# Output projection of a two-branch layer: token blocks 2 and 3 computed with seven block products in place of eight

## The chip, the cores and the metric

The kernel runs on one core of a Trainium2 chip. The core has a matrix engine (TensorE, PE in the profile; its weight loads are the row PEld), three engines for elementwise work (VectorE = DVE, ScalarE = ACT, GpSimd = POOL), a queue that issues transfers (SyncE = SP) and 16 DMA engines. SBUF is the on-chip working memory with 128 partitions; PSUM holds eight banks of 128 x 512 float32 values, into which TensorE accumulates. The metric is the device time of one execution in microseconds (us).

## The reference, cut to what matters

x has 2048 tokens of 640 channels. A linear-attention branch and an MLP branch read the same normalised x, and both are added to x.

```python
xn = _layernorm(x)
# branch A: q, k, v, two softmaxes per head, linear attention -> o (2048 x 640)
o = num / den
A = o.transpose(0, 2, 1, 3).reshape(B, S, D) @ wo          # wo: 640 x 640
# branch B: layernorm, 640 -> 1728, gelu, 1728 -> 640
return x + A + B_
```

The change lies in the product with `wo`, the last work of the kernel.

## The kernel before, in words

Tokens are handled in four blocks b = 0..3 of 512 columns, channels in KC = 5 bands of 128 partitions. Everything is kept transposed (channels on partitions, tokens along the row), so the projection is, for output band m of block b, the sum over bands c of `wo[c, m]` transposed times `o[c]`. Float32 accuracy is kept by splitting each operand into a high part, which has the reduced format float32r, and a low part, the rest. `mm3` (L70, L71, L72) issues the three products high x high, high x low and low x high for one pair of bands, each a 128 x 128 by 128 x 512 matmul. A column of the projection is one (b, m): five such triples, fifteen matmuls, into one PSUM bank; the columns use banks 6 and 7 in turn (`pw_`). VectorE then adds the bank to `acc[b][:, m]` (L1424), which holds x plus the MLP so far, and SyncE stores that column (L1425). The very last column is cut into two halves of 256 tokens.

The work just ahead of the projection is the end of the MLP: group g = 6, blocks 2 and 3, second matrix. There each output band takes five matmuls (L70 to L72 and L326, L327) into banks 5, 6, 7 in turn, and VectorE adds the bank to `acc` (L331). The fifth band of block 3 is the fourteenth use of this ring and takes bank 5 again, two uses after band 1 of block 3; the first projection column takes bank 6, which band 2 of block 3 held.

Four kinds of work run beside the projection:
- `Attention.split` makes the high part of a band on ScalarE (L1284) and its low part on VectorE (L1286). Block 0's and block 1's are made from `tf` tiles, blocks 2's and 3's from `acc` tiles.
- For block 3 the attention's quotients are still being finished: VectorE takes a reciprocal of `dt` (L1247), transfers spread it over the tile `rx` (L1248 to L1257), VectorE shuffles it (L1263) and GpSimd multiplies it into the result `ob` (L1265), band by band.
- The `acc` of blocks 0 and 1 comes back from memory (L1290) into the tiles that the splits have just read.
- In the last pass, `load_wo` fetches the high and low parts of `wo` (L1296, L1298).

What sets the order: PE, DVE, ACT and POOL run in the order in which the program emits their instructions (`manual_schedule`). The program emits along TensorE's work: after each triple it calls `mlp.tick()`, and a step registered with `mlp.after(n, ...)` is emitted n ticks later. A tick is thus a place in each engine's queue and no time: an engine goes on to its next instruction as soon as that one's data are there, however far TensorE has come. SyncE's queue alone is ordered by a planner from its own estimate of times.

Of the kernel before, what the change touches and what calls it, by code (L numbers as in the profile page):

```python
# [8 lines left out]
F32 = mybir.dt.float32  # L9
F32R = mybir.dt.float32r  # L10
AF = mybir.ActivationFunctionType
ALU = mybir.AluOpType
# [3 lines left out]
P = 128  # L16
S, D, F, H, DH = 2048, 640, 1728, 32, 20
KC = D // P
NB = S // 512
# [27 lines left out]
def f(ap):  # L47
    return ap.bitcast(F32)
# [3 lines left out]
def tile_kernel(ctx: ExitStack, tc: tile.TileContext, x, xT, wkT, wqT, wv, wphi, wo, w1, b1, w2, b2,  # L52
                ident, mmask, emask, vsel, out):
    nc = tc.nc
# [14 lines left out]
    def mm3(ps, lh, ll, rh, rl, first, last, **kw):  # L69
        nc.tensor.matmul(ps, lh, rh, start=first, stop=False, **kw)  # L70
        nc.tensor.matmul(ps, lh, rl, start=False, stop=False, **kw)  # L71
        nc.tensor.matmul(ps, ll, rh, start=False, stop=last, **kw)  # L72
# [25 lines left out]
    acc = [None] * NB  # L98
# [4 lines left out]
    banks = ctx.enter_context(tc.tile_pool(name="banks", bufs=1, space=PSUM))  # L103
# [13 lines left out]
    rp = ys.enter_context(tc.tile_pool(name="raw", bufs=1))  # L117
    wp = ys.enter_context(tc.tile_pool(name="w", bufs=1))

    def mtile(i, dtype=F32):  # L120
        return mp.tile([P, 2, D if i < 5 else 512], dtype, name=f"m{i}")
    y = {}

    def load_x(ts, xp, tag="xb"):
        xbs = []
        for t in ts:
            xb = xp.tile([P, D], F32, name=tag)
            nc.sync.dma_start(xb, x[t * P:(t + 1) * P, :])
            xbs.append(xb)
        return xbs  # L130
# [386 lines left out]
    mlp = Mlp((0, 1, 2, 3), ((0, 2), (1, 3)))  # L517
# [8 lines left out]
    x0 = load_x(range(2), xp)  # L526
    nc.sync.dma_start(idt, ident)
    wc, parts, dmas = {}, {}, {}
# [23 lines left out]
    x1 = load_x(range(4, 8), xp)  # L552
# [330 lines left out]
    a = ExitStack()  # L883
# [228 lines left out]
    t1 = sp.tile([VM, 5, 480], F32, name="t1")  # L1112
# [198 lines left out]
    wol, phs = [], []  # L1311
    ep = rx = None
# [20 lines left out]
    at = {}  # L1333
# [21 lines left out]
    ep = ctx.enter_context(tc.tile_pool(name="eB", bufs=1, side="right", reuse_waits="tile"))  # L1355
# [35 lines left out]
    w2t, parts = mlp.take_pair(6, True, 3)  # L1391
# [13 lines left out]
    finish(before)  # L1405
    load_ob(1)

    pw_ = Banks(6, 7)
    step = 0
    for b in range(NB):  # L1410
        oh, ol = at[b].oh, at[b].ol
        for m in range(KC):
            ms = slice(m * P, (m + 1) * P)

            for cols in [slice(0, 512)] if (b, m) != (NB - 1, KC - 1) else [slice(0, 256), slice(256, 512)]:
                pw = pw_()[:, cols]
                for c in range(KC):
                    mm3(pw, wol[0][c][:, ms], wol[1][c][:, ms], oh[:, c, cols], ol[:, c, cols], c == 0, c == KC - 1)
                    step += 1
                    mlp.tick()  # L1420
                    for n, at_ in enumerate((3, 28, 53), 1):
                        if step - at_ in range(KC + 1):
                            at[n].split(step - at_, nc.vector)
                nc.vector.tensor_tensor(acc[b][:, m, cols], pw, acc[b][:, m, cols], op=ALU.add)  # L1424
                nc.sync.dma_start(out[ms, b * 512 + cols.start:b * 512 + cols.stop], acc[b][:, m, cols])  # L1425


_INS = ["x", "xT", "wkT", "wqT", "wv", "wphi", "wo", "w1", "b1", "w2", "b2", "ident", "mmask", "emask", "vsel"]
# [60 lines left out]
```

## Time and profile before

| what | value |
|---|---|
| median of 3 runs | 713.96 us (712.85 to 714.65) |
| profiled execution, its own time | 713.46 us |
| its span, first to last instruction | 711.6 us |
| TensorE busy | 703.8 us, 99% of the span |
| DVE, ACT, POOL busy | 514.0, 342.0, 421.4 us |
| granted TensorE clock | 1.000 |
| projection: first matmul | 639.76 us from the span's start |
| last column added | 708.27 us |

The page's columns: a row of the timeline has the start in us from the span's start, the duration in us, the engine, the line, the operation, the tile written and the tiles read, the shapes, how many equal instructions are merged in the row, and in brackets how long the engine had been idle before it and what ended that. A busy TensorE is not TensorE at its peak, and a matmul's recorded duration overlaps the next; the distance between starts is its cost.

### The profile page before, as it was taken

The numbers are of one execution on the slowest core, as the hardware profiler recorded it, in microseconds if no ns is written. First come the engines' busy times: TensorE is split into PE (matmuls) and PEld (weight loads), VectorE is DVE, ScalarE is ACT, GpSimd is POOL, SyncE is SP. The second block draws the span as 40 slices with busy tenths as digits, with TensorE's granted clock in tenths as the row PEclk, the third lists the DMA queues.
The fourth block names the chain that finished last, engine by engine and source line by source line (L and its number), as shares of the span: only waits on it lengthen the run. The fifth ranks groups of instructions, "written<-read, shape, count | busy, mean of one in ns | idle before, by whom it ended". The sixth has DMA issues, their size and how long they took to land. (4 is left out here: it accounts for less than half of the span.)

```text
span 711.6 us, 9745 instructions
## 1 busy us (share of the span) xinstructions
PE 703.8 (99%) x3381; PEld 592.2 (83%) x3381; DVE 514.0 (72%) x821; ACT 342.0 (48%) x563; POOL 421.4 (59%) x360
## 2 busy tenths in 40 slices
PE   9999999999999999999999999999999999999998
PEld 7878888888888888888888888888887878888886
DVE  7777755988754788788888878657769695784622
ACT  6434554444334545545544546367665766450100
POOL 3521314577245997898787879468679787540400
PEclk9999999999999999999999999999999999999999
DMA  9823643485621228236401609964355568446222
GB/s 325 288 72 109 193 121 98 155 266 172 214 105 74 93 75 245 70 110 199 99 0 32 159 1 349 227 191 127 115 162 153 164 187 296 164 127 214 84 80 74
DMA packets 65767, 106.56 MB, mean 150 GB/s; under 512 B 7462, under 2 KB 31814, under 8 KB 63838
## 3 DMA queue, kind: packets, MB, share of 16 engines
q1 hardware_dynamic: 65414, 105.93, 46.5%
q8 instruction: 26, 0.43, 0.2%
q14 instruction: 23, 0.19, 0.1%
q10 hardware_dynamic: 304, 0.01, 0.0%
HBM read 71.37 MB, written 34.55 MB: 149 GB/s over the span
## 5 line engine op out<-in xcount | busy, mean ns | idle before, releaser
L906 PE MATMUL bank<-wkh,y 128*128 128x512 f32 (+1 forms) x480 | 139.5, 364 | 0.0
L70 PE MATMUL bank<-y,w 128*128 128x512 f32 (+1 forms) x294 | 114.2, 389 | 0.0
L71 PE MATMUL bank<-y,w 128*128 128x512 f32 (+1 forms) x294 | 113.7, 387 | 0.0
L72 PE MATMUL bank<-y,w 128*128 128x512 f32 (+1 forms) x294 | 113.6, 386 | 0.0
L64 POOL TENSOR_TENSOR w<-r,w 128x640 fp32r<-128x640 f32 x32 | 52.2, 1645 | 96.0 <-ACT w L61 67.0
L70 PE MATMUL bank<-m,w 128*128 128x512 f32 x260 | 102.3, 394 | 1.1 <-DVE acc L331 0.8
L71 PE MATMUL bank<-m,w 128*128 128x512 f32 x260 | 101.3, 390 | 0.9 <-DVE m L461 0.9
L72 PE MATMUL bank<-m,w 128*128 128x512 f32 x260 | 101.3, 390 | 0.0
L906 PEld LDWEIGHTS bank<-wkh,y 128*128 128x128 f32 x480 | 87.5, 188 | 13.3
L906 PE MATMUL bank<-wkl,y 128*128 128x512 f32 (+1 forms) x240 | 87.4, 364 | 0.0
L70 PEld LDWEIGHTS bank<-y,w 128*128 128x128 f32 x294 | 55.2, 188 | 11.7 <-issue 0.4
L72 PEld LDWEIGHTS bank<-y,w 128*128 128x128 f32 x294 | 55.2, 188 | 11.3
L71 PEld LDWEIGHTS bank<-y,w 128*128 128x128 f32 x294 | 55.2, 188 | 10.9
L942 ACT ACTIVATE m<-m,rs_all 128x1280 f32<-128x1280 f32 x32 | 43.7, 1365 | 42.9 <-POOL m L941 42.8
L70 PEld LDWEIGHTS bank<-m,w 128*128 128x128 f32 x260 | 48.8, 188 | 11.9 <-DVE acc L331 1.0
L944 DVE TENSOR_REDUCE sm<-m 128x64 f32<-128x1280 f32 x32 | 47.4, 1481 | 15.0 <-ACT m L942 14.8
L71 PEld LDWEIGHTS bank<-m,w 128*128 128x128 f32 x260 | 48.8, 188 | 11.1 <-DVE m L461 1.4
L906 PE MATMUL bank<-w,y 128*128 128x512 f32 x240 | 57.4, 391 | 0.0
L72 PEld LDWEIGHTS bank<-m,w 128*128 128x128 f32 x260 | 48.8, 188 | 10.2
L941 POOL TENSOR_TENSOR m<-m,mx 128x640 f32<-128x640 f32 (+2 forms) x48 | 44.4, 939 | 19.2 <-DVE mx L930 19.2
L331 DVE TENSOR_TENSOR acc<-bank,acc 128x512 f32<-128x512 f32 x70 | 46.9, 683 | 11.1 <-PE bank L72 5.9
L906 PEld LDWEIGHTS bank<-w,y 128*128 128x128 f32 x240 | 44.4, 188 | 8.5
(184 smaller groups left out, 1447.2 us busy)
## 6 DMA issues: line engine op xcount, KB each, us to landing
r<-in_w SPq DMA_DIRECT2D x52, 320.0 KB
e<-e SPq DMA_DIRECT2D x40, 256.0 KB
e<-acc SPq DMA_DIRECT2D x52, 160.0 KB
acc<-in_xT SPq DMA_DIRECT2D x4, 1280.0 KB
t<-t SPq DMA_DIRECT2D x8, 512.0 KB
tf<-t SPq DMA_DIRECT2D x2, 1536.0 KB
xb<-in_x SPq DMA_DIRECT2D x8, 320.0 KB
t<-in_x SPq DMA_DIRECT2D x8, 320.0 KB
```

Source lines behind the costliest of these rows:

```text
L64: eng.tensor_tensor(lo, src, f(hi), op=ALU.subtract)
L70: nc.tensor.matmul(ps, lh, rh, start=first, stop=False, **kw)
L71: nc.tensor.matmul(ps, lh, rl, start=False, stop=False, **kw)
L72: nc.tensor.matmul(ps, ll, rh, start=False, stop=last, **kw)
L331: nc.vector.tensor_tensor(acc[b][:, m, :], pw, acc[b][:, m, :], op=ALU.add)
L906: nc.tensor.matmul(ps, lh[:, kc, c], rh[:, kc], start=n == 0, stop=n == 3 * KC - 1)
L941: subs[n, t] = nc.gpsimd.tensor_tensor(ep[:, s], a, b, op=ALU.subtract)
L942: exps[n, t] = nc.scalar.activation(e, e, AF.Exp, scale=rs_all[:, t:t + 1])
L944: nc.vector.tensor_reduce(sm, e.rearrange("p s (h f) -> p (s h) f", f=DH), axis=AX, op=ALU.add)
```

## The change

Blocks 0 and 1 are projected as before. For blocks 2 and 3 the five bands are parted into four and one. The four input bands c = 2q + i and the four output bands m = 2k + j, with q, k, i, j in 0..1, make for each q and k a 2 x 2 block matrix out of `wo` (its blocks a11, a12, a21, a22; the first index is the output's parity, the second the input's), and the two token blocks make the 2 x 2 matrix b11 (block 2, even band), b21 (block 2, odd band), b12 and b22 (block 3). Its product is formed by the variant of Strassen's method with seven block products:

- sums of `wo`: s1 = a21 + a22, s2 = s1 - a11, s3 = a11 - a21, s4 = a12 - s2
- differences of the attention output ("turned forms"): t1 = b12 - b11, t2 = b22 - t1, t3 = b22 - b12, t4 = b21 - t2
- products a11 b11, a12 b21, s1 t1, s2 t2, s3 t3, a22 t4, s4 b22; the partial sums are kept in banks `a`, `b`, `c`, and a bank is read and added to `acc` at several stages of its accumulation.

The fifth input band is added by `rest` as one triple for each output column, and the fifth output band is a whole column as before, in two halves for block 3.

The new supporting work, with its ticks counted from the first triple of the projection:
- tick 1, `load_sums`: one transfer of 4 x 512 columns of `wo`, 1 MB, into tile `w1` (L1412).
- ticks 12 to 18, `add`: the four sums on GpSimd, in place in `w1` (L1424 of the new program, 512 elements in each partition).
- ticks 20 to 26, `hi_sum` and `lo_sum`: their high parts on ScalarE (L1427) and low parts on VectorE (L1431).
- ticks 42 to 60: eight differences on GpSimd (`combine`, L1440). For each, ScalarE writes the high part twice (`turn_hi`, L1456), once to SBUF and once to PSUM bank 3 or 4, and VectorE subtracts to get the low part (`turn_lo`, L1461), reading its first operand from that bank.
- Block 3's split begins at tick 59; before it began at 53.

Lines of the new program that stand for old ones: L1481 and L1518 for the addition L1424, L1482 and L1520 for the store L1425.

```diff
+    def load_sums():
+        sums.append(wp.tile([P, 4, D], F32, name="w1").rearrange("p i d -> p (i d)")[:, :4 * 512])
+        nc.sync.dma_start(sums[0].rearrange("p (c n) -> p c n", c=4), wo[:4 * P, :512].rearrange("(c p) n -> p c n", p=P))
...
+    def add(i):
...
+        o, x0, x1, op = ((a22, a21, a22, ALU.add), (a21, a11, a21, ALU.subtract), (a11, a22, a11, ALU.subtract), (a12, a12, a11, ALU.subtract))[i]
+        nc.gpsimd.tensor_tensor(o, x0, x1, op=op)
+    def hi_sum(c):
+        nc.scalar.activation(sums[1][:, c * 512:c * 512 + 512], sums[0][:, c * 512:c * 512 + 512], AF.Copy)
+    def lo_sum(o, w):
+        at_ = slice(o, o + w)
+        nc.vector.tensor_tensor(lo_part(o)[:, :w], sums[0][:, at_], f(sums[1][:, at_]), op=ALU.subtract)
...
+        nc.gpsimd.tensor_tensor(o, x0, x1, op=ALU.subtract)
...
+        bank = copies()
+        for o in (parts[0], bank):
+            nc.scalar.activation(o.rearrange("p (t q n) -> p t q n", q=4, t=4), src, AF.Copy)
...
+        nc.vector.tensor_tensor(lo, bank, f(hi), op=ALU.subtract)
...
+    steps = [(1, load_sums)]
+    steps += [(12 + 2 * i, lambda i=i: add(i)) for i in range(4)]
+    steps += [(20 + c, lambda c=c: hi_sum(c)) for c in range(4)]
...
+    for n, t in ((1, 3), (2, 28), (3, 59)):
+        steps += [(t + c, lambda n=n, c=c: at[n].split(c, nc.vector)) for c in range(KC + 1)]
+    for t, step in sorted(steps, key=lambda e: e[0]):
+        mlp.after(t, step)
...
+    for k in range(2):
+        place("a", k, k)
+        product("a", k, "a11", "b11", True)
+        read("a", k, 0, 2, False)
+        place("c", k, (2, 5)[k])
+        product("c", k, "a12", "b21", True)
+        rest("c", k, 0, 2)
+        read("c", k, 0, 2)
+    column(2, 4, [2])
+    for k in range(2):
+        place("b", k, (5, 2)[k])
+        product("b", k, "s1", "t1", True)
+        read("b", k, 1, 3, False)
+        product("a", k, "s2", "t2")
+        read("a", k, 0, 3, False)
+        place("c", k, (2, 5)[k])
+        product("c", k, "a22", "t4", True)
+        rest("c", k, 1, 2)
+        read("c", k, 1, 2, False)
+        product("a", k, "s3", "t3")
+        read("a", k, 1, 2)
+        product("b", k, "s4", "b22")
+        rest("b", k, 0, 3)
+        read("b", k, 0, 3)
+        rest("a", k, 1, 3)
+        read("a", k, 1, 3)
+    column(3, 4, [0, 5], (slice(0, 256), slice(256, 512)))
```

SyncE's queue near the end of the MLP, the difference between the two programs: `d`, `o` and `dt` are the denominators and late rows of block 3's attention, `w_6048` is the tile `w1` that takes `wo`.

```order
 L1240 DMA d_98<-acc_5547 4x2560
 L1240 DMA d_98<-acc_5547 2x2560
+L1412 DMA w_6048<-in_wo 128x4x512
 L1244 DMA acc_5547<-o_83 4x2560
 L1242 DMA dt<-d_98 128x128
```

The planner has put the load of `wo` between the two stores of the denominators and the loads that follow them; it waits only for the last matmul that read `w1` (L308 of block 3).

GpSimd's queue from the end of the MLP to its end: `m` is the last hidden tile of the MLP (L314), `acc_5165` and `acc_5547` are the results of blocks 2 and 3, `e` are free tiles.

```order
 L314 TENSOR_TENSOR m_5924<-m_5893,m_5924 64x512
 L1265 TENSOR_TENSOR acc_5165<-acc_5165,rx 128x512
-L1265 TENSOR_TENSOR acc_5547<-acc_5547,rx 128x512 x5
-L1485 UNCONDITIONAL_BRANCH
-L1485 ISA
+L1424 TENSOR_TENSOR w_6048<-w_6048 128x2x2x128 x4
+L1265 TENSOR_TENSOR acc_5547<-acc_5547,rx 128x512 x4
+L1440 TENSOR_TENSOR acc_5165<-acc_5547,acc_5165 128x512
+L1265 TENSOR_TENSOR acc_5547<-acc_5547,rx 128x512
+L1440 TENSOR_TENSOR acc_5165<-acc_5547,acc_5165 128x512
```

The four sums now stand directly behind the last product of block 2 and wait for the load alone; the differences stand among and behind the products of block 3.

VectorE's queue from the third column of block 1 on, before (`tf` is block 1's sum, `acc_4122` block 2's, `y` the split's parts):

```order
L1424 TENSOR_TENSOR tf_6086<-bank_6208,tf_6086 128x512
L1424 TENSOR_TENSOR tf_6086<-bank_6230,tf_6086 128x512
L1424 TENSOR_TENSOR tf_6086<-bank_6249,tf_6086 128x512
L1286 TENSOR_TENSOR y_6278<-acc_5547,y_6277 128x512 x2
L1424 TENSOR_TENSOR acc_4122<-bank_6267,acc_4122 128x512
L1286 TENSOR_TENSOR y_6278<-acc_5547,y_6277 128x512 x3
```

The same place now (`m` and `e` are the parts of the turned forms):

```order
L1481 TENSOR_TENSOR tf_6091<-bank_6226,tf_6091 128x512
L1481 TENSOR_TENSOR tf_6091<-bank_6248,tf_6091 128x512
L1461 TENSOR_TENSOR m_6267<-bank_6268,m_6267 128x512
L1461 TENSOR_TENSOR m_6283<-bank_6284,m_6283 128x512
L1461 TENSOR_TENSOR m_6296<-bank_6297,m_6296 128x512
L1481 TENSOR_TENSOR tf_6091<-bank_6273,tf_6091 128x512
L1461 TENSOR_TENSOR m_6311<-bank_6312,m_6311 128x512
L1518 TENSOR_TENSOR acc_4122<-bank_6307,acc_4122 128x512
L1461 TENSOR_TENSOR m_6325<-bank_6326,m_6325 128x512
L1518 TENSOR_TENSOR acc_4122<-bank_6321,acc_4122 128x512
```

The eight low parts of the turned forms stand between the additions of the columns, and block 3's split comes behind them.

More of the change, by code (lines that the diff above doesn't have):

```diff
@@ L1406, in tile_kernel @@
     load_ob(1)
[L1408 to L1411, printed above, removed]
-        for m in range(KC):
[L1413 to L1425, printed above, removed]
+    sums, turned = [], {}
@@ new lines, in lo_sum, with combine @@
+    def lo_sum(o, w):
+        at_ = slice(o, o + w)
+        nc.vector.tensor_tensor(lo_part(o)[:, :w], sums[0][:, at_], f(sums[1][:, at_]), op=ALU.subtract)
+    def combine(i, q):
+        c0, c1 = 2 * q, 2 * q + 1
+        x = {(b, c): at[b].ob[:, c] for b in (2, 3) for c in (c0, c1)}
+        t = {j: turned[j, q][0] for j in (1, 2, 3, 4) if (j, q) in turned}
+        o = ep.tile([P, 512], F32, name="e", bufs=6) if i in (2, 3) else x[2, c0 if i == 1 else c1]
+        x0, x1 = {1: lambda: (x[3, c0], x[2, c0]), 2: lambda: (x[3, c1], t[1]), 3: lambda: (x[3, c1], x[3, c0]), 4: lambda: (x[2, c1], t[2])}[i]()
+        nc.gpsimd.tensor_tensor(o, x0, x1, op=ALU.subtract)
+        turned[i, q] = [o]
@@ new lines, in tile_kernel, with turn_hi @@
+    copies = Banks(3, 4)
+    def turn_hi(i, q):
+        src = turned[i, q][0].rearrange("p (q t n) -> p t q n", q=4, t=4)
+        n = 2 * (i - 1) + q
+        if n == 7:
+            parts = [ep.tile([P, 512], F32, name="e", bufs=6).bitcast(F32R) for _ in range(2)]
+        else:
+            m = mtile(n, F32R)
+            parts = [m[:, p, :512] for p in range(2)]
+        bank = copies()
+        for o in (parts[0], bank):
+            nc.scalar.activation(o.rearrange("p (t q n) -> p t q n", q=4, t=4), src, AF.Copy)
+        turned[i, q] += [bank, parts]
@@ new lines, in tile_kernel, with column @@
+    for n, t in ((1, 3), (2, 28), (3, 59)):
+        steps += [(t + c, lambda n=n, c=c: at[n].split(c, nc.vector)) for c in range(KC + 1)]
+    for t, step in sorted(steps, key=lambda e: e[0]):
+        mlp.after(t, step)
+    def column(b, m, banks_of, parts=(slice(0, 512),)):
+        ms = slice(m * P, (m + 1) * P)
+        for n, cols in zip(banks_of, parts):
+            pw = banks.tile([P, 512], F32, name=f"bank{n}")[:, cols]
+            for c in range(KC):
+                mm3(pw, wol[0][c][:, ms], wol[1][c][:, ms], at[b].oh[:, c, cols], at[b].ol[:, c, cols], c == 0, c == KC - 1)
+                mlp.tick()
+            nc.vector.tensor_tensor(acc[b][:, m, cols], pw, acc[b][:, m, cols], op=ALU.add)
+            nc.sync.dma_start(out[ms, b * 512 + cols.start:b * 512 + cols.stop], acc[b][:, m, cols])
@@ new lines, in tile_kernel, with place, left @@
+    for b in range(2):
+        for m in range(KC):
+            column(b, m, [6 + (b + m) % 2])
+    places = {}
+    def place(n, k, i):
+        places[n, k] = banks.tile([P, 512], F32, name=f"bank{i}")
+    def left(n, p, q, k):
+        i, j = {"a11": (0, 0), "a12": (1, 0), "a22": (1, 1), "s1": (1, 1), "s2": (0, 0), "s3": (0, 1), "s4": (1, 0)}[n]
+        c, o = 2 * q + i, (2 * k + j) * P
+        if n[0] == "a":
+            return wol[p][c][:, o:o + P]
+        return sums[1][:, c * 512 + o:c * 512 + o + P] if p == 0 else lo_part(c * 512 + o)[:, :P]
@@ new lines, in right, with product, rest @@
+    def right(n, q):
+        if n[0] == "t":
+            return turned[int(n[1]), q][2]
+        i, j = int(n[1]) - 1, int(n[2]) - 1
+        return [z[:, 2 * q + i] for z in (at[2 + j].oh, at[2 + j].ol)]
+    def product(n, k, l, r, start=False):
+        for q in range(2):
+            mm3(places[n, k], left(l, 0, q, k), left(l, 1, q, k), *right(r, q), start and q == 0, q == 1, skip_group_check=True)
+            mlp.tick()
+    def rest(n, k, i, b):
+        ms = slice((2 * k + i) * P, (2 * k + i + 1) * P)
+        mm3(places[n, k], wol[0][4][:, ms], wol[1][4][:, ms], at[b].oh[:, 4], at[b].ol[:, 4], False, True, skip_group_check=True)
+        mlp.tick()
@@ new lines, in read @@
+    def read(n, k, i, b, last=True):
+        m = 2 * k + i
+        nc.vector.tensor_tensor(acc[b][:, m], places[n, k], acc[b][:, m], op=ALU.add)
+        if last:
+            nc.sync.dma_start(out[m * P:(m + 1) * P, b * 512:(b + 1) * 512], acc[b][:, m])
+    for k in range(2):
[6 more added lines that the diff above has]
+        read("c", k, 0, 2)
```

11 lines of the change are left out of this document (added).

## The prediction

> **What bounds the kernel now.** I read the page first, then the chain of work that ended last, then the timelines of single engines around the projection.
>
> ```profile
> PE 703.8 (99%) x3381; PEld 592.2 (83%) x3381; DVE 514.0 (72%) x821; ACT 342.0 (48%) x563; POOL 421.4 (59%) x360
> PEclk9999999999999999999999999999999999999999
> ```
>
> TensorE is busy for 99% of the span at the full granted clock in all 40 slices. The chain says the same for the last stage:
>
> ```profile
> 639.79 0.43 PE bank L70
> ...
> 708.27 0.42 DVE acc L1424
> ```
>
> From the first triple of the projection to the last addition it goes along TensorE. So a matmul less is time gained, and a wait of TensorE is time lost; other engines count where TensorE waits for them. The pace, from TensorE's timeline and VectorE's additions:
>
> ```profile
> 638.50 0.39 PE L70 MATMUL bank<-m,w 128*128 128x512 f32 x1
> ...
> 639.40 0.39 PE L327 MATMUL bank<-m,w 128*128 128x512 f32 x1
> 639.76 0.47 PE L70 MATMUL bank<-y,w 128*128 128x512 f32 x1
> ```
>
> ```profile
> 650.28 0.69 DVE L1424 TENSOR_TENSOR tf<-bank,tf 128x512 f32<-128x512 f32 x1 [2.37 <-PE bank L72]
> 653.68 0.69 DVE L1424 TENSOR_TENSOR tf<-bank,tf 128x512 f32<-128x512 f32 x1 [2.71 <-PE bank L72]
> ```
>
> A column of fifteen matmuls takes 653.68 - 650.28 = 3.40 us, so one matmul 0.227 and a triple 0.68. The one irregular step is 639.40 to 639.76: 0.36 where 0.23 is the pace. Here the projection's first column waits for VectorE to empty bank 6. VectorE at that place:
>
> ```profile
> 633.03 0.69 DVE L331 TENSOR_TENSOR acc<-bank,acc 128x512 f32<-128x512 f32 x1 [0.44 <-PE bank L327]
> 634.16 0.69 DVE L331 TENSOR_TENSOR acc<-bank,acc 128x512 f32<-128x512 f32 x1 [0.44 <-PE bank L327]
> 634.77 0.68 DVE L1286 TENSOR_TENSOR y<-tf,y 128x512 fp32r<-128x512 f32 x1
> 635.37 0.68 DVE L331 TENSOR_TENSOR acc<-bank,acc 128x512 f32<-128x512 f32 x1
> 635.97 1.28 DVE L1286 TENSOR_TENSOR y<-tf,y 128x512 fp32r<-128x512 f32 x2
> 637.17 0.68 DVE L331 TENSOR_TENSOR acc<-bank,acc 128x512 f32<-128x512 f32 x1
> 637.77 1.28 DVE L1286 TENSOR_TENSOR y<-tf,y 128x512 fp32r<-128x512 f32 x2
> 638.97 1.88 DVE L331 TENSOR_TENSOR acc<-bank,acc 128x512 f32<-128x512 f32 x3
> 640.77 0.94 DVE L1247 RECIPROCAL dt<-dt 128x128 f32<-128x128 f32 x1
> ```
>
> From 634.16 on VectorE works without a pause, one instruction each 0.60 us, with the five low parts of block 0 (L1286) among the additions of block 3. The addition at 637.17 frees bank 5 for the fifth band (at 638.50, 0.65 us in hand); the one at 638.97 frees bank 6 for the projection, and is already late by that 0.13. VectorE has no slack here, and what delays those five L1286 delays TensorE.
>
> **Removed.** Blocks 2 and 3 had 4 x 4 x 2 = 32 triples outside the fifth bands; seven products for two q and two k make 28. Four triples are 12 matmuls: 12 x 0.227 = 2.72 us, all on the path. This is the whole possible gain, 0.38%.
>
> **Added: the load and the sums of `wo`.** GpSimd and SyncE before:
>
> ```profile
> 631.56 1.29 POOL L314 TENSOR_TENSOR m<-m,m 64x512 fp32r<-64x512 f32 x1 [3.21 <-DVE acc L331]
> 632.93 1.30 POOL L1265 TENSOR_TENSOR acc<-acc,rx 128x512 f32<-128x512 f32 x1
> ```
>
> ```profile
> 628.60 1.16 SPq L1240 DMA_DIRECT2D d<-acc  x2
> 630.99 0.52 SPq L1244 DMA_DIRECT2D acc<-o  x1
> ...
> 639.09 0.32 SPq L1290 DMA_DIRECT2D tf<-a  x1
> ```
>
> ```profile
> 427.25 1.05 SPq L512 DMA_DIRECT2D acc<-in_xT  x2
> ```
>
> ```profile
> 427.30:432.30 5.00, 5.00 (x29) 4.34 (x28) 5.00 (x6) 4.11 (x8) 5.00 (x4) 1.00 0.70 208
> 630.00:639.00 9.00, 9.00 (x42) 7.44 (x41) 7.51 (x14) 6.57 (x12) 2.59 (x2) 1.00 0.06 19
> ```
>
> The load stands behind the two L1240 and waits for the matmul just ahead of the MLP's last ten bands (ten times five matmuls, 11.3 us before 639.6, so done near 628.5); it is issued at 628.60 + 1.16 = 629.8. A load of the same kind, 2 KB pieces from an input, issued at 427.25, moved 5.00 x 208 GB/s = 1.04 MB, the size wanted, by 432.3: 5.0 us. The 1.31 MB of L1290, issued at 639.09, held VectorE's addition until 644.82 (row below), 5.7 us, or 4.6 in proportion to the bytes. The DMA engines were nearly idle from 630 to 639 (last column: 19 GB/s). So `wo` lands at 634.4 to 634.8; I take 634.5. The loads L1244 and L1242 come behind it, some 3 us later than before, and the reciprocal that needs them stands at 640.77: no cost.
>
> ```profile
> 644.82 0.69 DVE L1424 TENSOR_TENSOR tf<-bank,tf 128x512 f32<-128x512 f32 x1 [1.97 <-DMA tf<-a]
> ```
>
> GpSimd is free at 632.93 + 1.30 = 634.23, and its tick keeps no sum back. So the four sums, 512 elements each like L1265, run from 634.5, among VectorE's L1286. What happens then is shown by an MLP group, VectorE first, then GpSimd:
>
> ```profile
> 482.85 1.34 DVE L461 TENSOR_TENSOR m<-m,m 128x512 fp32r<-128x512 f32 x1
> 484.12 2.05 DVE L393 TENSOR_TENSOR w<-s,w 128x768 fp32r<-128x768 f32 x1
> ```
>
> ```profile
> 482.07 1.58 POOL L393 TENSOR_TENSOR w<-r,w 128x640 fp32r<-128x640 f32 x1 [0.20 <-ACT w L392]
> 483.61 1.75 POOL L1208 TENSOR_TENSOR e<-e,m 128x512 fp32r<-128x512 f32 x1
> 485.31 2.29 POOL L393 TENSOR_TENSOR w<-r,w 128x640 fp32r<-128x640 f32 x1
> ```
>
> L461 reads two SBUF tiles, as L1286 does, and is recorded with 1.34 us, not 0.68: GpSimd's operation ended at 483.65, and L461 ended 0.54 later. GpSimd's next one, some 1.3 long by itself, ended at 485.36, and VectorE's next ended 0.81 after that; the third, 1.58 by itself, took 2.29. They take turns: whoever waits comes next, and neither gets two turns while the other waits. An addition from a bank has one tile in SBUF and is not held: the L331 at 633.03 ran in 0.69 inside GpSimd's 632.93 to 634.23.
>
> Step by step, 1.28 for a sum and 0.60 for VectorE. Sum 1: 634.5 to 635.8. L1286 number 1 waits for it, ends 636.4; L331 (band 0) 637.0. Sum 2 to 637.7; L1286 number 2 to 638.3. Sum 3 to 639.6; number 3 to 640.2; L331 (band 1) 640.8. The fifth band starts at 640.9 in place of 638.50: 2.4 late. Sum 4 to 641.5; numbers 4 and 5 to 642.7; L331 (band 2) 643.3. The projection starts at 643.4 in place of 639.76: 3.65 us lost in all, counting the first wait. The same walk gives 3.4 for a landing before 634, up to 4.6 for one at 636, 2.0 to 2.6 for 637 to 638, nothing after 638.4: ends 0 and 4.6.
>
> Each restart of TensorE costs a little more, by the longest wait of an MLP group:
>
> ```profile
> 550.41 0.39 PE L70 MATMUL bank<-m,w 128*128 128x512 f32 x1
> 551.75 0.50 PE L71 MATMUL bank<-m,w 128*128 128x512 f32 x1 [0.95 <-DVE m L461]
> 552.08 0.40 PE L72 MATMUL bank<-m,w 128*128 128x512 f32 x1
> ```
>
> 551.75 to 552.08 is 0.33 for 0.23: 0.1 each, 0.2 for two. TensorE stood idle for 1.1 us there, and the granted clock stayed full. [...]
>
> What follows the projection's late start moves with it: L1290 waits for the last L1286 (now 642.7) and lands near 648.4; the third column needs that addition at 643.4 + 6.8 = 650.2.
>
> **Added: high parts and low parts of the sums, reads.** ScalarE's 20 new activations at 0.54 (the row below: 2.72 for 5) have its idle 20.5 us behind it; the low parts of the sums, two us, stand in VectorE's idle 2.71 per column; the eight more additions, at 0.69, have at least three triples, 2.04, between a bank's read and its next use. Nothing each; without that cover 0.7 per addition.
>
> ```profile
> 657.12 2.72 ACT L1284 ACTIVATE y<-acc 128x512 fp32r<-128x512 f32 x5 [20.49 <-PE bank L72]
> ```
>
> **Added: the turned forms.** GpSimd at the end before, and the group's mean:
>
> ```profile
> 665.60 2.54 POOL L1265 TENSOR_TENSOR acc<-acc,rx 128x512 f32<-128x512 f32 x2 [0.18 <-DVE rx L1263]
> ...
> L1265 POOL TENSOR_TENSOR acc<-acc,rx 128x512 f32<-128x512 f32 x20 | 27.9, 1404 | 26.9 <-DVE rx L1263 26.4 <-DMA e<-e 0.4
> ```
>
> Block 1 began at 656.8 here; call it B. The fourth product ended at 666.9, B + 10.1. Nine operations follow now in place of one: at 1.27 by their spacing, B + 21.5, or B + 23 where block 2's L1286, now in another order, take turns with the products. Behind the last come two activations (1.1), its low part, an L1286 and the addition that frees bank 5 (0.69, 0.60, 0.69): B + 24.6 to 26.1. Product b needs bank 5 at B + 40 x 0.68 = B + 27.2. Four more L1286 and an addition (3.1) free bank 2 by B + 29.2, needed at B + 29.9. So it just holds, with 1.1 and 0.7 us in hand, and costs nothing at these prices. At 1.40 each, the group's mean, thirteen operations (four products too) come 1.7 later, 1.0 beyond the smaller slack; at 1.45 it is 1.6. A wait can give no gain, so the ends are 0 and 1.6; I take 0.3, near the lower end, since that mean contains the turns. [...]
>
> **Sum.** 713.46 - 2.72 + 3.65 + 0.2 + 0.3 = 714.9 against the profiled execution, which lies 0.5 below the median of 713.96; from the median it would be 715.4. The runs before spread over 1.8 us; I say 715.0, a little slower, and within the 0.3% (2.1 us) which is about what a measurement of this kernel can tell from no change.
>
> **Rivals.** (1) Slower by more: GpSimd's chain is late for bank 5 and bank 2. Point: 0.06 us more for each of the thirteen operations uses up the smaller slack. With 1.45 per operation the sums of `wo` cost 4 x 0.17 = 0.7 more and the turned forms 1.6: 714.9 + 0.7 + 1.6 - 0.3 = 716.9. For it: so little slack at the end of a chain of 16 us. Against: the spacing of 1.27. (2) Faster: the sums miss block 0's L1286 (landing after 638.4, or VectorE served first): 713.46 - 2.72 = 710.7, from the median 711.2. Against: idle DMA engines, and the turns at 483. (3) A landing at 637 to 638: 2.0 to 2.6 lost, 713.2 to 714. (4) The granted clock falls at a wait. [...] Against: the full clock after 1.1 us idle.
>
> **How the numbers follow.** My forecast 0.45; rival 1 with what else makes it slower by over 0.3% 0.30; rival 2 0.15; rival 3 0.07; rival 4 0.03. Faster by over 0.3%: 0.15. Within: 0.45 + 0.07 = 0.52. Slower: 0.33. The range 711.0 to 717.2 holds the forecast, rival 3, most of rivals 1 and 2; the forecast's own is 713.9 to 716.1.
>
> **What would show it.** TensorE: two waits ahead of the projection, 2.4 and 1.3 us, on VectorE; four GpSimd operations from about 634.5 among L1286 of over 1 us; then an even pace with 12 matmuls fewer. Wrong if `wo` lands late, if VectorE is not held, or if TensorE waits for bank 5 or bank 2 behind block 1.

## The result, and the profile after

| | before | after |
|---|---|---|
| median of 22 executions, us | 713.75 (712.26 to 715.46) | 715.87 (713.00 to 717.78) |
| ratio, 95% interval | | 1.0028 (1.0018 to 1.0038) |
| matmuls | 3381 | 3369 |
| profiled execution, us (span) | 713.46 (711.6) | 713.00 (711.2) |

The kernel became 0.28% slower by the ratio. The medians lie 2.1 us apart, where 12 matmuls fewer should have gained 2.7. The profiled execution of after is the fastest of its 22, so it shows only a part of the loss. I begin with that part.

TensorE after, its timeline at the place where the projection begins:

```profile
637.38 0.39 PE L327 MATMUL bank<-m,w 128*128 128x512 f32 x1
638.67 0.50 PE L70 MATMUL bank<-m,w 128*128 128x512 f32 x1 [0.90 <-DVE acc L331]
639.01 0.40 PE L71 MATMUL bank<-m,w 128*128 128x512 f32 x1
...
639.71 0.40 PE L327 MATMUL bank<-m,w 128*128 128x512 f32 x1
642.08 0.47 PE L70 MATMUL bank<-y,w 128*128 128x512 f32 x1 [1.98 <-ACT w L1427]
642.39 0.39 PE L71 MATMUL bank<-y,w 128*128 128x512 f32 x1
```

Before, this stretch had one irregular step of 0.36 us. Now it has two waits. From 637.38 to 638.67 is 1.29 against a pace of 0.23, so 1.06 are lost ahead of the fifth band. From 639.71 to 642.08 another 2.15 are lost ahead of the projection. Two slow restarts (0.34 and 0.31 in place of 0.23) add 0.19. That makes 3.40, against 0.21 at the same place before (0.13 for the wait, 639.40 to 639.76, and 0.08 for its restart, 639.76 to 640.07): 3.19 more. The row at 642.08 names ScalarE, but the bank was VectorE's to free:

```profile
633.89 0.68 DVE L1286 TENSOR_TENSOR y<-tf,y 128x512 fp32r<-128x512 f32 x1
634.49 0.69 DVE L331 TENSOR_TENSOR acc<-bank,acc 128x512 f32<-128x512 f32 x1
635.09 2.93 DVE L1286 TENSOR_TENSOR y<-tf,y 128x512 fp32r<-128x512 f32 x2
637.94 0.68 DVE L331 TENSOR_TENSOR acc<-bank,acc 128x512 f32<-128x512 f32 x1
638.54 2.84 DVE L1286 TENSOR_TENSOR y<-tf,y 128x512 fp32r<-128x512 f32 x2
641.30 1.87 DVE L331 TENSOR_TENSOR acc<-bank,acc 128x512 f32<-128x512 f32 x3
```

GpSimd and SyncE at the same place:

```profile
634.48 6.35 POOL L1424 TENSOR_TENSOR w<-w 128x512 f32<-128x512 f32 x4 [1.14 <-PE bank L327]
```

```profile
628.90 0.39 SPq L1412 DMA_DIRECT2D w<-in_wo  x1
```

Two L1286 take 2.93 and 2.84 us where two took 1.28 before. GpSimd's four sums began at 634.48. (Their row names TensorE as what ended the wait before it; in e2 and e3, below, the same wait ends with the load.) They take 6.35 where they take 5.45 in e2, in which VectorE's operations beside them read a bank. The first two sums and the first two held low parts, one by one:

```profile
634.48 1.30 POOL L1424 TENSOR_TENSOR w<-w 128x512 f32<-128x512 f32 x1 [1.14 <-PE bank L327]
635.86 1.62 POOL L1424 TENSOR_TENSOR w<-w 128x512 f32<-128x512 f32 x1
```

```profile
635.09 1.24 DVE L1286 TENSOR_TENSOR y<-tf,y 128x512 fp32r<-128x512 f32 x1
636.25 1.77 DVE L1286 TENSOR_TENSOR y<-tf,y 128x512 fp32r<-128x512 f32 x1
```

The sums end at 635.78 and 637.48, the low parts 0.55 and 0.54 behind them: one low part for each sum, every 1.7 us. While the sums run, an addition from a bank (L331 at 637.94) keeps its 0.68. When the addition at 637.94 has read bank 5, the fifth band starts; when the first of the three at 641.30 has read bank 6, the projection starts.

Behind 642.4 TensorE waits no more. The turned forms, GpSimd and then VectorE:

```profile
670.62 1.29 POOL L1440 TENSOR_TENSOR acc<-acc,acc 128x512 f32<-128x512 f32 x1
...
679.38 2.58 POOL L1440 TENSOR_TENSOR e<-acc 128x512 f32<-128x512 f32 x2
```

```profile
684.38 0.68 DVE L1518 TENSOR_TENSOR acc<-bank,acc 128x512 f32<-128x512 f32 x1
684.99 2.48 DVE L1286 TENSOR_TENSOR y<-acc,y 128x512 fp32r<-128x512 f32 x4
687.39 0.68 DVE L1481 TENSOR_TENSOR acc<-bank,acc 128x512 f32<-128x512 f32 x1
```

```profile
686.38 0.39 PE L70 MATMUL bank<-m,w 128*128 128x512 f32 x1
...
689.11 0.39 PE L70 MATMUL bank<-m,w 128*128 128x512 f32 x1
```

GpSimd issues the nine operations 1.25 us apart and is done at 681.96. VectorE has read bank 5 at 685.06, 1.3 ahead of its next matmul at 686.38, and bank 2 at 688.07, 1.0 ahead of 689.11.

So in this execution the projection's account is -2.72 + 3.19 = +0.47. It was 0.46 shorter all the same, because it came to the projection 0.9 earlier (L1240 is issued at 627.70, before at 628.60). That is chance: the MLP groups have short waits that come and go. Before's first profile has one of 1.1 us at 551, which no other profile has, before's second (e7) included. A wait of 0.8 near 580 stands in all of them, the two first profiles too.

The rest of the loss is in the list of executions, in TensorE's mean granted clock. Before's 27 executions measured beside the experiments all had 1.000 or 0.999. After's 22:

| mean granted clock | executions | time, us | median, us |
|---|---|---|---|
| 1.000 | 3 | 713.00 to 713.35 | 713.18 |
| 0.997 to 0.998 | 11 | 713.93 to 717.00 | 715.67 |
| 0.994 | 8 | 716.19 to 717.78 | 717.40 |

In 19 of 22 executions the clock fell somewhere. That is the open question for the experiments, together with the proof that GpSimd's sums cause the two waits.

### The profile page after: what moved, and what is told of

It is laid out like the page before. It is cut to its first block, busy times and chain, and to the rows that moved or that the text cites. A ratio compares the mean times of both kernels' runs of the same rounds, so it can differ in the third digit from the quotient of the medians.

```text
span 711.2 us, 9789 instructions
## 1 busy us (share of the span) xinstructions
PE 701.3 (99%) x3369; PEld 589.5 (83%) x3369; DVE 530.6 (75%) x842; ACT 353.0 (50%) x583; POOL 436.3 (61%) x372
## 4 chain that ended last, share of the span: by engine, by line
PE 91%; DVE 3%; issue 2%; DMA 2%; POOL 1%; ACT 0%; SPq 0%; DVEq 0%; POOLq 0%; ACTq 0%
PE bank L906 28%; PE bank L70 18%; PE bank L72 18%; PE bank L71 18%; PE bank L976 3%; PE bank L644 2%; DMA r<-in_w 2%; PE bank L1214 1%; PE bank L1215 1%; POOL w L64 1%; PE bank L307 1%; PE bank L308 1%; DVE y L1286 1%; PE bank L1146 1%; PE bank L327 0%
## 5 line engine op out<-in xcount | busy, mean ns | idle before, releaser
L70 PE MATMUL bank<-m,w 128*128 128x512 f32 x274 | 108.0, 394 | 2.0 <-DVE acc L331 1.7
L70 PE MATMUL bank<-y,w 128*128 128x512 f32 (+1 forms) x274 | 106.4, 388 | 2.0 <-ACT w L1427 2.0
L71 PE MATMUL bank<-m,w 128*128 128x512 f32 x274 | 106.7, 389 | 0.0
L71 PE MATMUL bank<-y,w 128*128 128x512 f32 (+1 forms) x274 | 105.9, 386 | 0.0
L72 PE MATMUL bank<-y,w 128*128 128x512 f32 (+1 forms) x270 | 104.3, 386 | 0.0
L72 PE MATMUL bank<-m,w 128*128 128x512 f32 x262 | 102.0, 389 | 0.0
L70 PEld LDWEIGHTS bank<-m,w 128*128 128x128 f32 x274 | 51.5, 188 | 14.1 <-DVE acc L331 2.7
L70 PEld LDWEIGHTS bank<-y,w 128*128 128x128 f32 x274 | 51.5, 188 | 12.9 <-ACT w L1427 2.4
L71 PEld LDWEIGHTS bank<-m,w 128*128 128x128 f32 x274 | 51.4, 188 | 10.4 <-DVE m L461 0.2
L71 PEld LDWEIGHTS bank<-y,w 128*128 128x128 f32 x274 | 51.5, 188 | 10.2
L72 PEld LDWEIGHTS bank<-y,w 128*128 128x128 f32 x270 | 50.7, 188 | 10.3
L72 PEld LDWEIGHTS bank<-m,w 128*128 128x128 f32 x262 | 49.2, 188 | 10.3
L331 DVE TENSOR_TENSOR acc<-bank,acc 128x512 f32<-128x512 f32 x70 | 47.0, 683 | 10.7 <-PE bank L72 5.6
L64 DVE TENSOR_TENSOR m<-m,m 128x512 fp32r<-128x512 f32 (+1 forms) x34 | 26.7, 792 | 33.7 <-ACT m L61 33.7
```

Of the source, the lines that this page charges most:

```text
L64: eng.tensor_tensor(lo, src, f(hi), op=ALU.subtract)
L331: nc.vector.tensor_tensor(acc[b][:, m, :], pw, acc[b][:, m, :], op=ALU.add)
```

## The experiments

**e1: the changed kernel again**, no edit.

> The changed kernel once more, beside the next three on the same chip. The theory says: two waits of TensorE ahead of the projection, 1.1 and 2.2 us beyond the pace, and a granted clock that in most executions falls for a while behind them: a mean of 0.997 to 0.998 costs about 1.5 to 2 us of 711, one of 0.994 about 4. So an execution with a mean clock of 1.000 takes 713.0 to 713.5 us, one with 0.998 about 715, one with 0.994 about 717; the median lies 1.5 to 2.5 us above before's. If the profiled execution has a mean clock below 1, the low clock begins behind the second wait, at about 640 us from the span's start, and not elsewhere. The rival, that the slower executions owe it to something else (transfers, the turned forms, chance), says: the low clock stands at other places, or the times do not go by the clock.

Measured: 716.37 (714.81 to 717.08, 6 runs) against 714.03 for before, ratio 1.0029 (1.0018 to 1.0041). The mean clock was 0.998 in four executions and 0.994 in two; the profiled one had 0.998 and 715.97 us. Its stretches around the projection, one row each: length, busy time and number of instructions of PE, PEld, DVE, ACT and POOL, then the granted clock, the DMA share and GB/s.

```profile
637.56:640.97 3.41, 2.39 (x11) 1.68 (x10) 3.41 (x4) 0.00 (x0) 3.25 (x3) 1.00 0.00 0
640.97:644.38 3.41, 1.42 (x7) 0.89 (x6) 3.41 (x5) 2.30 (x4) 1.26 (x1) 1.00 0.24 33
644.38:647.80 3.42, 3.42 (x10) 2.67 (x9) 2.21 (x4) 0.00 (x0) 0.00 (x0) 0.50 0.87 357
647.80:651.21 3.41, 3.41 (x16) 2.82 (x16) 2.42 (x4) 0.00 (x0) 0.00 (x0) 1.00 0.29 101
```

The waits are there again, 1.18 and 2.15 us, the second from 641.3 to 643.5. Then, from 644.38 to 647.80, the clock is halved and ten matmuls touch the window in place of sixteen (eight start in it, at full clock fifteen). It is the only low stretch ahead of the last matmul. The first profile, with the same wait but full clock, cut on the same grid of 3.413 us:

```profile
636.94:640.35 3.41, 2.27 (x9) 1.23 (x7) 3.41 (x4) 0.16 (x1) 3.25 (x3) 1.00 0.00 0
640.35:643.77 3.42, 1.69 (x7) 1.42 (x8) 3.42 (x6) 2.14 (x4) 0.48 (x1) 1.00 0.33 84
643.77:647.18 3.41, 3.41 (x17) 2.82 (x16) 1.45 (x4) 0.00 (x0) 0.00 (x0) 1.00 0.78 320
```

Here the grid cuts the long wait (639.9 to 642.1) in two, and no window is as empty as e1's second. Two more profiles of the changed kernel came later:

> The changed kernel, a third profile. By the rule read from the stretch of pauses (the clock is set per window of 3.413 us; a window with less than 40% of its full work, six matmuls of fifteen, is followed by one at half clock), stepped through the recorded starts of the changed kernel's matmuls at every phase of the grid, 22% of the executions have no low window (about 713.2 us), 60% one (1.65 us more), 18% two (2.9 more), and none has more. Each low window costs 1.7 us where TensorE works all through it. The low windows lie between 640 and 648 us from the span's start. A rival: that the executions with a mean clock of 0.994 have low windows elsewhere too, at waits that this profile has not yet shown.

> The changed kernel, a fourth profile, with the same expectation: none, one or two windows of 3.413 us at half clock with chances of 22, 60 and 18%, all of them between 640 and 648 us from the span's start and none elsewhere, and before each of them a window in which fewer than six matmuls ran.

They took 716.27 and 715.77 us, and each had one low window of 3.413 us, from 644.07 and from 643.32, behind a window that held the whole wait of 2.15 and a third of its work. Their first waits were 1.01 and 0.52. Four profiles of after thus have none, one, one and one. In all 30 executions of after, 3 have a full clock, 17 a mean of 0.997 or 0.998 and 10 one of 0.994. Two low windows alone would give 0.995.

The rest of a 0.994 can be a fall that costs no time. Behind its last matmul TensorE is idle while the last column is added and stored, and a low stretch can begin before the execution ends. In e4's profile this is the only one, and its mean is 0.999:

```profile
703.73:707.14 3.41, 0.96 (x9) 0.76 (x7) 0.42 (x1) 0.00 (x0) 0.00 (x0) 1.00 0.23 77
707.14:708.05 0.91, 0.00 (x0) 0.00 (x0) 0.00 (x0) 0.00 (x0) 0.00 (x0) 0.50 0.00 0
```

If the limit that e6 shows is stepped through after's matmuls to the end of the execution (at 0.40, every phase of the grid), nine in ten of the phases with two low windows have such a stretch too, and then the mean is 0.994. This is an estimate; no profile caught a 0.994.

**e2: the low parts of block 0 by way of PSUM.** The load, the sums and all else stay.

```diff
             if c < KC:
                 nc.scalar.activation(parts(self.oh[:, c, :]), tokens(self.ob[:, c, :]), AF.Copy)
+                if b == 0:
+                    self.copied = getattr(self, "copied", []) + [mlp.px()]
+                    nc.scalar.activation(parts(self.copied[c]), tokens(self.ob[:, c, :]), AF.Copy)
-            if c:
+            if c and b == 0:
+                eng.tensor_tensor(self.ol[:, c - 1, :], self.copied[c - 1], f(self.oh[:, c - 1, :]), op=ALU.subtract)
+            elif c:
```

> The changed kernel, but the low parts of block 0 are made by way of PSUM as those of the turned forms are: ScalarE writes one more, unrounded copy of each band to bank 3 or 4, and VectorE subtracts with one operand in that bank. The load of wo and GpSimd's four sums stay where they are. If VectorE was held because its five operations and GpSimd's sums both read two tiles of SBUF: those five run in 0.6 to 0.7 us each, the sums in 1.28 each, TensorE has no wait above 0.3 us ahead of the projection, the granted clock stays at 1.000 in nearly all executions, and the time is before's less 2.4 to 2.8 us, about 711.0. If the load's 1 MB of writes into SBUF held VectorE, or the sums hold it wherever it reads, the waits of 1.1 and 2.2 us stay, and the time is that of the changed kernel, before plus 0.5 to 2.5 us.

Measured: 710.75 (709.64 to 712.24, 5 runs) against 714.03, ratio 0.9953 (0.9940 to 0.9965), clock 1.000 in all five. GpSimd, VectorE and TensorE of this kernel (L1429 are the sums, L1289 block 0's low parts):

```profile
634.86 5.45 POOL L1429 TENSOR_TENSOR w<-w 128x512 f32<-128x512 f32 x4 [1.49 <-DMA w<-in_wo]
```

```profile
634.94 1.28 DVE L1289 TENSOR_TENSOR y<-bank,y 128x512 fp32r<-128x512 f32 x2
636.14 0.68 DVE L331 TENSOR_TENSOR acc<-bank,acc 128x512 f32<-128x512 f32 x1
636.74 1.29 DVE L1289 TENSOR_TENSOR y<-bank,y 128x512 fp32r<-128x512 f32 x2
637.94 1.88 DVE L331 TENSOR_TENSOR acc<-bank,acc 128x512 f32<-128x512 f32 x3
```

```profile
638.38 0.39 PE L327 MATMUL bank<-m,w 128*128 128x512 f32 x1
638.72 0.47 PE L70 MATMUL bank<-y,w 128*128 128x512 f32 x1
```

The sums run at the same place, but VectorE's operations keep 1.28 for two, and the step at the projection is 0.34, as before. What held VectorE in after was thus its two operands in SBUF beside GpSimd's sums, not the load and not the sums by themselves: two low parts took 2.93 beside the sums there, and 1.28 here with one operand in PSUM. In this run too the next low part with both operands in SBUF (L1291, at 639.73) took 1.12 beside the last sum, and ended 0.54 after it (640.85 and 640.31). With one change more, this version keeps the whole gain of the seven products and is faster than both kernels.

**e3: the load on ScalarE's queue, later.**

```diff
-        nc.sync.dma_start(sums[0].rearrange(...), wo[:4 * P, :512].rearrange(...))
+        nc.scalar.dma_start(sums[0].rearrange(...), wo[:4 * P, :512].rearrange(...))
-    steps = [(1, load_sums)]
+    steps = [(9, load_sums)]
```

> The changed kernel, but wo is loaded through ScalarE's queue behind block 1's high parts, not through SyncE's: it is issued some 6 us later and lands at about 641 us, so that GpSimd's sums come behind block 0's five low parts. The theory of the collision says: no wait of TensorE above 0.3 us ahead of the projection, no fall of the clock, and the time is before's less 2 to 2.8 us, about 711.2. GpSimd is then some 6 us later with the sums and the differences behind them, which stand 1.0 us or more ahead of bank 2's and bank 5's next use: if they wait for the sums and not for block 3's quotients, up to 4 us of wait appear at the products with bank 5 in the middle of the second half. The rival, that the sums cost TensorE the same wherever they stand, says before plus 0.5 to 2.5 us.

My premise failed: the transfer stood ahead of the high parts in ScalarE's queue and was issued at 630.04, so the sums began only 1.7 us later than in after, measured from the last matmul ahead of the fifth band. That made it a half dose:

```profile
636.30 6.05 POOL L1424 TENSOR_TENSOR w<-w 128x512 f32<-128x512 f32 x4 [2.87 <-DMA w<-in_wo]
```

```profile
635.17 1.29 DVE L1286 TENSOR_TENSOR y<-tf,y 128x512 fp32r<-128x512 f32 x2
636.38 0.69 DVE L331 TENSOR_TENSOR acc<-bank,acc 128x512 f32<-128x512 f32 x1
636.98 2.88 DVE L1286 TENSOR_TENSOR y<-tf,y 128x512 fp32r<-128x512 f32 x2
```

Two low parts are held in place of four, TensorE has one wait of 1.72 us in place of two, and the time is 712.39 (711.23 to 715.48, 10 runs), ratio 0.9978 (0.9965 to 0.9990). The account is -2.72 + 1.72 - 0.13 = -1.1; measured -1.6 (-2.5 to -0.7). The clock was 0.999 or 1.000 in nine of ten executions, and 0.998 in the one of 715.48. The turned forms brought no wait.

**e4: no sums.** The line of `steps` with `add(i)` is left out, so four of the seven products use unsummed blocks.

> The changed kernel without GpSimd's four sums of wo: the load stays, its high and low parts are made from the unsummed blocks, and the products with s1 to s4 use those, so that only the form of the work is kept. The theory of the collision says: no wait ahead of the projection, clock 1.000, before less 2.4 to 2.8 us, about 711.0; what it lacks to 2.72 is the cost of all the rest. If the load alone delays VectorE or TensorE, the waits stay in part; if the clock falls in most executions without the waits, the cause of the fall lies elsewhere in the changed kernel (its fifteen-matmul columns broken up, its reads of banks), and the median stays above before's less 1 us.

Measured: 710.66 (709.84 to 712.68, 5 runs), ratio 0.9955 (0.9941 to 0.9968). VectorE has before's rows again although the load runs:

```profile
635.18 1.28 DVE L1286 TENSOR_TENSOR y<-tf,y 128x512 fp32r<-128x512 f32 x2
...
636.98 1.29 DVE L1286 TENSOR_TENSOR y<-tf,y 128x512 fp32r<-128x512 f32 x2
```

The load alone costs nothing that can be seen, and neither do the turned forms, the eight more additions and ScalarE's activations: they are all in this kernel, and it is 3.2 us (2.3 to 4.2) below before, where 2.72 is the whole gain of the matmuls. The clock was 1.000 or 0.999 in four of five executions and 0.998 in one.

**e5: the side work alone.** The load, the sums and their high and low parts, with eight products for all blocks:

```diff
-    for n, (i, q) in enumerate((i, q) for i in (1, 2, 4, 3) for q in range(2)):
-        steps += [(42 + 2 * n, lambda i=i, q=q: combine(i, q)), ...]
...
-    for b in range(2):
+    for b in range(NB):
         for m in range(KC):
-            column(b, m, [6 + (b + m) % 2])
+            if (b, m) != (NB - 1, KC - 1):
+                column(b, m, [6 + (b + m) % 2])
+    column(3, 4, [7, 6], (slice(0, 256), slice(256, 512)))
```

> Only the side work of the change: the load of wo, GpSimd's four sums and their high and low parts stand where the changed kernel has them, but nothing reads them; all four blocks are projected with eight block products, as before, and there are no turned forms. If the sums among block 0's low parts are the whole price of the change: two waits of TensorE ahead of the projection, 1.1 and 2.2 us, as in the changed kernel, 3.2 us in all beyond before's 0.2, and a clock that falls for one or more stretches of 3.4 us in most executions, 1.7 us each. The time is before plus 3.2 in an execution with a full clock, and before plus 4.5 to 6 in the median, a ratio of 1.0065 to 1.008; that is the changed kernel plus 2.5 to 3. If the turned forms or the seven products have a part in the fall of the clock or in the price, the ratio is 1.004 or less and the clock full.

Measured: 717.91 (716.14 to 720.04, 6 runs) against 713.82, ratio 1.0062 (1.0046 to 1.0078): 4.4 us more by the ratio, just below the 4.5 to 6 that were expected. In the profiled execution the waits are 0.52 and 2.15, and a low window follows:

```profile
639.17:642.59 3.42, 1.44 (x7) 0.96 (x6) 3.42 (x5) 1.25 (x3) 2.69 (x2) 1.00 0.25 51
642.59:646.00 3.41, 3.41 (x10) 2.64 (x9) 2.01 (x4) 1.05 (x3) 0.00 (x0) 0.50 0.85 352
```

Four of its six executions had a mean clock of 0.995 or 0.997, two 1.000. So the clock falls without the seven products, where the waits are. The clock alone does not order these six times: the two executions with 1.000 took 716.14 and 717.99.

**e6: which waits lower the clock.** Before's kernel with this stretch behind its last column:

```diff
+    def pause(bank, halves):
+        for o in range(0, halves, 2):
+            cols = slice(0, 256 * min(2, halves - o))
+            nc.vector.tensor_tensor(dst[:, cols], bank[:, cols], other[:, cols], op=ALU.subtract)
+    for i in range(40):
+        pause(burst(40 + 7 * i % 16), 1 + 3 * i % 10)
+    for i in range(12):
+        pause(burst(40 + 5 * i % 16), 1)
+        pause(burst(5), 3)
```

> The kernel before, with a stretch added behind its last column: TensorE runs bursts of 40 to 55 equal matmuls, and between two bursts it waits for one to ten half operations of VectorE (about 0.8 to 3.5 us), forty times; then twelve times a short wait, five matmuls and a wait of about 1.5 us, as the changed kernel has ahead of the projection. The question is which waits make the granted clock fall. Theory one, from the second profile of the changed kernel (a fall of 3.413 us that began behind a wait of 2.15 us, and none in the first, whose 2.15 us were cut in two by the same grid): the clock is set once per window of 3.413 us on a fixed grid, from how much of the window before TensorE worked; less than some share between 0.37 and 0.49 halves the next window. Then waits of under 1.7 us by themselves never bring a fall, waits of 1.8 to 3.4 us do if they lie in one window, that is with a chance that grows with their length, and two short waits can together. Theory two, that a whole window must be idle: no wait of under 3.4 us brings a fall. Theory three, that any wait above a length brings it, wherever it lies: falls behind all waits above about 2 us and behind none below. The time is before's plus about 600 us.

All low stretches of the trace are one or two windows of 3.413 us, 21 stretches with 25 windows, and all lie on one grid of that length. I cut the added stretch into the windows of this grid and took as TensorE's work what is left of a window without the gaps between matmuls beyond the pace. Of the windows at full clock:

| work, share of the window | windows | followed by one at half clock |
|---|---|---|
| 0.05 to 0.37 | 18 | 18 |
| 0.38 to 0.42 | 5 | 3 |
| 0.45 to 0.50 | 7 | 0 |
| 0.50 and more | 162 | 0 |

One pair with a fall and one without, each window and the next. The busy times count every matmul to its modelled end; by the pace the first window has 0.37 of its work and the third 0.46:

```profile
1251.89:1255.30 3.41, 1.44 (x7) 1.16 (x7) 1.81 (x3) 0.00 (x0) 0.00 (x0) 1.00 0.00 0
1255.30:1258.71 3.41, 3.41 (x10) 2.64 (x9) 0.00 (x0) 0.00 (x0) 0.00 (x0) 0.50 0.00 0
...
729.65:733.06 3.41, 1.81 (x9) 1.20 (x8) 1.38 (x2) 0.00 (x0) 0.00 (x0) 1.00 0.00 0
733.06:736.47 3.41, 3.41 (x17) 2.80 (x16) 0.00 (x0) 0.00 (x0) 0.00 (x0) 1.00 0.00 0
```

In this run the limit lies near 0.4 of a window, six matmuls of its fifteen. Of the 25 low windows the four that were followed by another low one were busy for 0.52 to 0.77 of their time, at half clock 0.26 to 0.39 of the full work; the other 21, with 0.41 or more, were followed by full clock. So the same limit fits them. Theory one holds for this run. Theory two falls (longest idle stretches of 1.5 to 3.3 us in windows with a fall, none of a whole window), and so does theory three: 2.07 us idle in a window with 0.39 of work brought no fall, and in a window with 0.40 two waits, neither over 1.50, did.

**e7: before again**, no edit.

> The kernel before, unchanged, for a second profile of it. Its first had a wait of 1.1 us in an MLP group at 551 us, which none of the four profiles of variants with the same work up to 620 us has, the changed kernel among them. If that wait comes and goes with the execution, it may be missing here, and the time is then about 712.3; if it belongs to this program, it is here again, and part of the variants' gain over before is owed to its absence. Clock 1.000.

One execution of 715.27 us, clock 1.000. The wait at 551 is missing and one of 0.15 at 620 is there; the 0.8 near 580 is in both profiles of before. This execution was already 2.7 us later than the first at 530. The wait at 551 comes and goes; that the time would be 712.3 without it was wrong. Single executions of one kernel differ by 2 to 3 us ahead of the projection, so the accounts above go by the waits and not by single totals.

## Why the prediction was right, and where it was wrong

The time was forecast as 715.0 and came out at 715.87, inside the range and inside the 0.3%. That it came so close is in part luck: the collision and the turned forms were put about 1.0 us too dear, and the clock, which the sum put at nothing, cost about 1.5.

- **Removed, 2.72 us: right.** From the last matmul ahead of the projection to the last of all before takes 68.55 us (639.40 to 707.95) and e2 65.80 (638.38 to 704.18): 2.75 less, with nearly the same step at the projection. In the medians e2 and e4 lie 3.4 (2.5 to 4.3) and 3.2 (2.3 to 4.2) below before, which includes 2.7.
- **The sums collide with block 0's low parts: right in place and kind, too large.** Start on GpSimd, the turns, both banks and both waits came as written. The load was issued as forecast (628.90, in an execution 0.9 earlier than before's), but the sums began 5.6 us after that, not 4.7. One low part slipped through and four were held in place of five. The loss is 3.19 with restarts where 3.65 + 0.2 were put. The term that was too large is the turn: the walk put 1.28 + 0.60 = 1.88 for a sum and a low part, and the sums end 1.7 us apart. The prediction's own rows had that size, 483.65 to 485.36 = 1.71 from one end of GpSimd's to the next. Walked from the start that occurred, 1.88 would have given 3.85, more and not less. e3 agrees: its sums began where rival 3 has them (637.1 by before's clock), and the wait was 1.72 where 2.0 to 2.6 were priced. The waits also stood the other way round: 1.06 first and 2.15 second, where 2.4 and 1.3 were forecast; in four profiles of after the first is 0.52 to 1.18 and the second always 2.15.
- **Turned forms, 0.3: they cost nothing.** The forecast of slack was 1.1 and 0.7; measured 1.3 and 1.0. GpSimd's products and block 2's low parts did take turns (two L1286 took 2.38 beside the product at 661.42, where two take 1.28 alone), so with B = 659.19 bank 5 came free at B + 25.9, near the later of the two ends forecast (24.6 and 26.1), and bank 2 at B + 28.9 (29.2). The spacing of 1.25 held. Rival 1 did not occur.
- **Load, activations, reads at nothing: right** (e4).
- **The step that failed is the clock, rival 4, with a chance of 0.03.** Against it stood "the full clock after 1.1 us idle". That is right and says little: in e6 a wait counts by what it leaves of a window. A wait of 2.15 leaves 1.26, or 0.37 of the window, under e6's limit of about 0.4; one of 1.1 leaves 0.68. The forecast's own first wait of 2.4 could have gone under the limit too (it leaves 0.30 of a window), so its sizes allowed a fall for which its sum has no term. By estimate a low window costs up to 1.7 us, half of its 3.41: in e1 eight matmuls start in it where fifteen do at full clock, and seven of 0.227 are 1.6. I stepped e6's limit (0.40) through the recorded matmuls of after's first profile, at 400 phases of the grid: 22% of the phases have no low window, 60% one (1.65 us), 18% two (2.9). The mean is 1.5. Measured over 30 executions: 10% full, 57% with one window's worth, 33% below. The kind agrees. That the low clock is more frequent than this gives is at the edge of what 30 executions can tell, and the first wait is not the same in each; this stays open.

With what was measured the sum closes: 713.75 - 2.72 + 3.19 + 1.5 = 715.7, against a median of 715.87. That the clock's part needs the waits is shown by e2, where they are gone and the clock is full in all five executions; that it does not need the seven products is shown by e5. One execution of e3 and one of e4 had 0.998 all the same, and where their clock fell was not seen. That the part's size is 1.5 is worked out and not measured by itself. The groups of executions agree with it only in part: from 0.998 to 0.994 the median rises by 1.73, one low window, but the three executions with a full clock have 713.18 where 714.2 would follow from -2.72 + 3.19. That 1.0 us is not explained.

The direction rested on one thing: VectorE and GpSimd had both to read two tiles at the place where VectorE had no slack. Rival 2, the sums that miss the low parts, was priced at 710.7 to 711.2. No profile of after was so, but e2 shows that this is what the change is worth without the collision: 710.75.

## What to carry to other kernels

Before work is added on GpSimd, look at which operations of VectorE with two tiles in SBUF stand beside it, and whether TensorE waits for VectorE there. If so, feeding one of VectorE's operands from PSUM took the whole collision away here (e2: 1.28 us for two low parts in place of 2.93, and a step of 0.34 at the projection), for one more copy by ScalarE, which had the time. Starting the added work 1.7 us later took away about half (e3: one wait of 1.72 in place of 1.06 and 2.15). And price a wait of TensorE by what it leaves of a window of 3.413 us. Three of the four profiles of after have a low window behind the wait of 2.15, worth up to 1.7 us by estimate; the fourth, where the grid cuts that wait in two, has none. In e6 two waits in one window, neither over 1.50, brought a fall too.

## What the hardware showed that I had not expected

In these traces TensorE's granted clock fell to 0.50 in windows of 3.413 us (e6: 25 of them, all on one grid), and the grid lies elsewhere in each execution: in after's first profile it cuts the wait of 2.15 in two, in e1's that wait lies in one window. In e6 a window with 0.37 and less of its full work was followed by one at half clock in 18 of 18 cases, with 0.38 to 0.42 in 3 of 5, with 0.45 and more in 0 of 169. The low windows fit the same limit if their work counts half: the four that another one followed had 0.26 to 0.39. So a kernel with nearly the same two waits in each execution has times in three groups, with medians of 713.2, 715.7 and 717.4 us, the last two overlapping. No window had to be empty for a fall: in e1, e8 and e9 the one ahead of it held about a third of its work.
